# A long convolution with routed experts on one core: fewer half transforms beside the first sort, the rest among the tile tables, rows ahead of the 48-point inputs

## The chip, the core and the metric

The kernel runs on one core of a Trainium2 chip. TensorE (PE), VectorE (DVE), ScalarE (ACT) and GpSimd (POOL) compute, each with an instruction queue of its own; SyncE (SP) issues most of the transfers, GpSimd issues those whose rows are given by a list of indices. The metric is the device time of one execution in microseconds; the lower the better.

## The reference

The input `x` has 8 batches of 5696 positions with 128 channels. Each is convolved with one long filter `h`, and every resulting row goes to the one of 8 experts that its gate prefers:

```python
Yf = np.fft.rfft(x, n=2 * S, axis=1) * np.fft.rfft(h, n=2 * S, axis=0)[None]
y = np.fft.irfft(Yf, n=2 * S, axis=1)[:, :S, :]
...
expert_idx = np.argmax(logits, axis=1)
for e in range(E):
    xe = x[expert_idx == e]
    out[expert_idx == e] = gate_w[expert_idx == e, None] * (np.maximum(xe @ w1[e], 0.0) @ w2[e])
```

Here the rows of `y` are the `x` of the second part, `logits = x @ w_gate`, and an expert has 1024 hidden channels.

## The kernel before

The convolution is a transform in two steps. The first ("half transforms", `phase_a`, tiles `pa`) mixes 120 blocks of a batch by a cosine and a sine matrix and leaves its result in a DRAM tensor `U`; an item is four of 48 columns of one batch, it is split into two float32r parts by ScalarE and VectorE (`xc`), has two halves (cosine, sine) of three matmuls each, and each half is copied out of PSUM to `ut` (one by ScalarE, one by VectorE). Three batches complete one pair of `U` stores. The second step (`phase_b`, 48-point, tiles `xp`, `vp`) takes 120 bins one by one: inputs `uq` from `U`, a matmul forward (`xp`), the product with the filter on VectorE (`zt`, `xs`), a sum (`combine`), and a matmul back (`vp`). `phase_c`, called the sort here, finishes the inverse transform (`lb` in the first group, `yp`), turns the rows (`tp`), scores them (`gb`), ranks them within their expert (`lmax` to `pi`, all on VectorE) and scatters them with GpSimd (`SR<-rt,pi`, line 686) into `SR`, the rows sorted by expert. After each scatter GpSimd clears a scratch tile (`spent`, line 919) in all steps but the last `QUICK`; nothing reads what the clearing writes leave there. `tables` computes, in small VectorE instructions on one partition, which 256 rows of `SR` make up each expert tile (`tab`).

The batches form three groups of 2, 3 and 3. `experts` goes through the tiles of 256 rows: SP reads a tile's place from `tab` and loads its rows (`xr`, line 1126) and, where the expert changes, weights (`wb`, line 1154); TensorE turns the rows (`mx`), multiplies them in four steps by the first weights (`mh`) and the second (`ma`), and GpSimd scatters the result to `out`. The first group's rows make up tiles 0 to 36; tile 37 is the first that needs rows of the second group. Rows are loaded up to three tiles ahead, and only when all scatters of their group are done.

The order of the instructions is planned in the program: `run` advances several generators in step, each with the cost that it yields, divided by its share in `SHARES`. Two stages matter here. In the first, the sort of group 0 (`gather`) runs beside `phase_a` of group 1 (`SHARES[1]`) and the preparation of weights. In the second, `experts` runs beside `rest()` (share 0.75), which goes on with `phase_b`, sort and so on of groups 1 and 2. A generator that yields `None` waits until another has moved on. In `rest()` the pieces of the first table stand two by two behind each bin of `phase_b`, and `begin`, which marks the group's rows as ready, comes when the bins have cost `HEAD[1]`. `LULL` holds the experts for a moment at their start. `ALONE` says for how many bins VectorE, not GpSimd, does the sum.

Of the kernel before, what the change touches and what calls it, by code (L numbers as in the profile page):

```python
# [44 lines left out]
F3 = (False, False, True, False)  # L45
MIX = 2
LD = 4
SHARES = (0.42, 0.195, 0, 0.75, 0.998, 0.42)
GAP = 5000
ALONE = (0, 14, 10)  # L50
HEAD = (0, 5500, 9000)
A3 = (True, True, True, True)
ALO = ('gpsimd', 'vector', 'vector', 'vector')
AT = 650
WARM = 4
TURN = (1, 1, 1, 1)
LULL = 2800
RARE = 3
STEP = 1065
XR = 19  # L60
PACE = (1800, 2200)
ROOM = 28
REST = (224, 288, 288)
QUICK = (1, 1, 24)
TABLED = 4
RATE = (0.372, 0.55, 0.28, 0.8, 1.05, 0.6)

# [2 lines left out]
def conv_moe(ctx: ExitStack, tc: tile.TileContext, I, out, B, S, D, E, F, split):  # L70
# [39 lines left out]
    class Part:  # L110
        def __init__(self, gr, s, b0, nb, c0, tiles):
            self.gr, self.g, self.s, self.b0, self.nb, self.c0 = gr, gr.g, s, b0, nb, c0
            self.cols = nb * D
            self.ni = SLOTS[gr.g] // nb
            while NB % self.ni:
                self.ni -= 1
            self.ns = self.ni * nb
            self.cb = 3 if self.ns % 3 == 0 else 2
            self.cw = self.cb * D
            self.nt = tiles  # L120
            self.ready = False
            self.ends = []
            self.sets = 2 if b0 + nb == B else 1

# [13 lines left out]
    groups, parts = [], []  # L138
# [314 lines left out]
    def phase_b(gr):  # L453
        g, cb, cw, nch, QB, PK = gr.g, gr.cb, gr.cw, gr.nch, gr.qb, gr.pk
# [187 lines left out]
            filt(1, k)  # L642
        for n in range(CUT):
            cut(n)
        for n in range(N + lags[3] + 2):
            qb, at = divmod(n, per)
            for k0 in range(at * PK, (at + 1) * PK):
# [88 lines left out]
    def phase_c(pt, guest=None):  # L736
# [6 lines left out]
        nu = NB // NI  # L743
# [196 lines left out]
        for n in range(n_end + 1):  # L940
            for k in range(nsub):
# [14 lines left out]
                lift(at + 2)  # L956
                if guest:
                    guest.begin(1 if k == nsub - 1 and n >= 1 else 2)
                yield cost if n < nu or pt is parts[-1] else cost / 2
                if guest:  # L960
                    guest.end()
                if n < nu:
# [118 lines left out]
    def begin(pt):  # L1081
        for _ in pt.pieces:
            pass
        pt.ends = lanes[-PIPE_LANES:] + pt.ends
        pt.ready = True

# [22 lines left out]
    def experts():  # L1109
# [118 lines left out]
        def tiles(lo, hi):  # L1228
# [2 lines left out]
            hss, wants, due = {}, [], [lo]  # L1231

            def pump():
                while wants and seq[wants[0][0]][0].ready:
                    load_w(*wants.pop(0))

            def want(i, n):
# [9 lines left out]
                    load(due[0])  # L1247
                    due[0] += 1

            while not seq[lo][0].ready:  # L1250
                yield None
            for n in range(4):
                want(lo, n)
            ahead(lo + 2)
            if lo == 0:
                yield LULL
            M = len(steps)
            for n in range(M + LAG + 1):
                j, k = steps[n] if n < M else (None, None)
# [44 lines left out]
    def gather(pt, guest=None):  # L1304
# [15 lines left out]
        state["space"] = False  # L1320
        yield 0

    def chain(*gens):
        for x in gens:
            yield from x

    def rest():
        wait = [groups[0].parts[-1]]
        for gr in groups[1:]:
            spent = 0  # L1330
            guest = Guest(groups[gr.g + 1]) if gr.g + 1 < len(groups) else None
            bins = phase_b(gr)
            for n, cost in enumerate(bins):
                if guest and n == QN * gr.nch - 12:
                    guest.start()
                spent += cost
                yield cost
                if wait:
                    for _ in range(2):
                        next(wait[0].pieces, None)  # L1340
                    if spent > HEAD[gr.g]:
                        begin(wait.pop())
            for pt in gr.parts:
                yield from gather(pt, guest)
            if guest:
                yield from guest.rest()
                wait.append(gr.parts[-1])
# [26 lines left out]
    with tc.manual_schedule():  # L1374
# [7 lines left out]
        sb.close()  # L1382
        sb.open("c")
        state["rests"] = False
        run((chain(*[gather(pt) for pt in g0.parts]), 1.0), (phase_a(groups[1]), SHARES[1]), (prep, SHARES[5]))
        sb.close()
        sb.close()
        sb.open("sb")
        run((experts(), 1.0), (back, SHARES[3]))
        sb.close()  # L1390


# [76 lines left out]
```

## Time and profile before

| | us |
|---|---|
| device time, median of 3 runs | 2142.5 (2141.74 to 2143.13) |
| the profiled execution | 2141.9, with a span of 2140.1 |
| TensorE busy | 2061.8 (96%) |
| VectorE busy | 1563.6 (73%) |
| GpSimd busy | 1293.2 (60%) |
| ScalarE busy | 1121.1 (52%) |

The span is the time from the first to the last instruction on the core; the device time has a little more around it. TensorE's busy time counts a slow matmul with its full length, so time at the lower clock looks busy.

### The profile page before, as it was taken

To read this page: it belongs to the slowest core of one execution; us is meant where nothing else is said; L and a number is where in the kernel's file an instruction comes from. 1 tells how busy PE (TensorE), PEld (TensorE's weight loads), DVE (VectorE), ACT (ScalarE), POOL (GpSimd) and SP (SyncE) were. 2 spreads that over 40 slices of the span, in tenths; PEclk is the share of its full clock that TensorE was granted. 3 is DMA by queue.
4 is the path that set the end of the run, shared out by engine and by line. 5 is a ranking of instruction groups with operands and counts; after the bars stand their busy time and mean duration, and the time that the engine had idled before them with its cause. 6 is when DMAs were issued, how large, how long until landed. Compare 5 with 4: busy or idle time off the path is not lost.

```text
span 2140.1 us, 47237 instructions
## 1 busy us (share of the span) xinstructions
PE 2061.8 (96%) x14548; PEld 1786.5 (83%) x14548; DVE 1563.6 (73%) x3523; ACT 1121.1 (52%) x2333; POOL 1293.2 (60%) x1431
## 2 busy tenths in 40 slices
PE   9999999799999999989999999999989999999998
PEld 6898777467777777768888888888889999999998
DVE  5688677799998687888888887677774555555554
ACT  5677555155555444435666665444444444444444
POOL 6566388645554288888998776166663444444333
PEclk9999999699999999989999999999999999999999
DMA  8999799889996898868778775656533244443331
GB/s 265 265 274 290 224 305 294 248 208 235 245 241 186 224 282 261 265 153 224 186 188 221 192 192 154 168 135 162 142 101 118 69 130 134 133 132 128 123 122 34
DMA packets 213409, 409.33 MB, mean 191 GB/s; under 512 B 31605, under 2 KB 135339, under 8 KB 213156
## 3 DMA queue, kind: packets, MB, share of 16 engines
q1 hardware_dynamic: 184975, 350.70, 58.6%
q0 software_dynamic: 27072, 55.35, 9.0%
q8 instruction: 118, 1.93, 0.4%
q14 instruction: 135, 1.11, 0.2%
q10 hardware_dynamic: 1109, 0.23, 0.1%
HBM read 571.44 MB, written 154.27 MB: 339 GB/s over the span
## 4 chain that ended last, share of the span: by engine, by line
PE 75%; DVE 7%; DMA 6%; POOL 5%; issue 3%; ACT 2%; SPq 1%; POOLq 0%; DVEq 0%; ACTq 0%
PE mh L164 21%; PE ma L164 21%; PE vp L164 8%; PE xp L164 8%; PE yp L164 4%; POOL SR L686 3%; PE pa L164 3%; PE mx L189 3%; DMA SR<-rt,pi 2%; DMA wb<-WD 1%; POOL spent L919 1%; PE lb L189 1%; PE hp L164 1%; DMA mt<-mq 1%; PE tp L189 1%
## 5 line engine op out<-in xcount | busy, mean ns | idle before, releaser
L1193 DVE SCALAR_TENSOR_TENSOR hs<-mh,hs 128x512 fp32r<-128x512 f32 x728 | 500.7, 689 | 363.0 <-ACT hs L1191 356.8
L164 PE MATMUL mh<-xtb,wb 128*128 128x256 f32 x4368 | 702.9, 296 | 21.6 <-DMA wb<-WD 10.3
L1191 ACT ACTIVATE hs<-mh 128x512 fp32r<-128x512 f32 x728 | 435.4, 598 | 465.6 <-PE mh L164 459.7
L164 PEld LDWEIGHTS mh<-xtb,wb 128*128 128x128 f32 x4368 | 587.2, 189 | 92.1 <-issue 39.3
L164 PE MATMUL ma<-hs,wb 128*128 128x256 f32 x4368 | 656.6, 286 | 7.3 <-DMA wb<-WD 7.2
L164 PEld LDWEIGHTS ma<-hs,wb 128*128 128x128 f32 x4368 | 571.9, 190 | 9.4 <-DMA wb<-WD 9.3
L686 POOL DMA_INDIRECT SR<-rt,pi x384 | 399.2, 1040 | 235.1 <-issue 71.4
L704 POOL DMA_INDIRECT out<-xr x308 | 302.5, 982 | 347.4 <-ACT hs L1191 177.2
L583 POOL TENSOR_TENSOR zt<-zt,xs 128x384 f32<-128x384 f32 (+1 forms) x276 | 295.6, 1073 | 154.3 <-DVE xs L573 74.5
L577 DVE TENSOR_TENSOR xs<-xp,hh 64x384 f32<-64x384 f32 (+1 forms) x360 | 214.7, 596 | 7.8
L620 ACT COPY vt<-vp 96x384 f32<-96x384 f32 x240 | 114.1, 475 | 197.2 <-PE vp L164 191.4
L164 PE MATMUL vp<-zt,mi 128*96 128x384 f32 x480 | 200.2, 499 | 2.0 <-PE xp L164 0.9
L568 DVE TENSOR_TENSOR zt<-xp,hh 128x384 f32<-128x384 f32 (+1 forms) x300 | 173.5, 578 | 31.3 <-PE xp L164 23.2
L164 PE MATMUL xp<-uq,mt 96*128 96x384 f32 (+1 forms) x496 | 175.7, 458 | 8.0 <-DMA uq<-U 4.0
L164 PE MATMUL pa<-xc,fcr 120*120 120x512 f32 x576 | 159.2, 411 | 2.0 <-POOL xc L296 1.0
L164 PE MATMUL yp<-vq,gcs 120*120 120x384 f32 x384 | 140.2, 486 | 2.0 <-ACT ut L329 2.0
L573 DVE SCALAR_TENSOR_TENSOR xs<-xp,hh 64x384 f32<-64x384 f32 x240 | 134.2, 559 | 4.2
L164 PEld LDWEIGHTS vp<-zt,mi 128*96 128x96 f32 x480 | 79.2, 166 | 51.0 <-issue 26.0
L164 PEld LDWEIGHTS pa<-xc,fcr 120*120 120x120 f32 x576 | 99.1, 185 | 25.6 <-DVE rk L908 3.3
L164 PEld LDWEIGHTS xp<-uq,mt 96*128 96x128 f32 x496 | 87.6, 200 | 32.1 <-issue 11.1
L329 DVE COPY ut<-pa 120x512 f32<-120x512 f32 x96 | 65.7, 684 | 64.6 <-PE pa L164 54.8
L557 POOL TENSOR_TENSOR us<-uq,us 96x384 fp32r<-96x384 f32 x81 | 83.0, 1025 | 30.6 <-ACT us L555 29.8
(166 smaller groups left out, 2591.5 us busy)
## 6 DMA issues: line engine op xcount, KB each, us to landing
wb<-WD SPq DMA_DIRECT2D x728, 512.0 KB
U<-ut SPq DMA_DIRECT2D x48, 720.0 KB
uq<-U SPq DMA_DIRECT2D x60, 576.0 KB
V<-vt SPq DMA_DIRECT2D x60, 576.0 KB
vq<-V SPq DMA_DIRECT2D x48, 720.0 KB
xt<-x SPq DMA_DIRECT2D x96, 240.0 KB
xr<-SR SPq DMA_DIRECT2D x154, 130.0 KB
WD<-wsp SPq DMA_DIRECT2D x32, 512.0 KB
```

The source lines that it names most:

```text
L164: nc.tensor.matmul(to, lhs, rhs, **kw)
L189: nc.tensor.transpose(dst, src, ident[:n, :n])
L557: eng.tensor_tensor(out=uv[:, 1], in0=src, in1=uv[:, 0].bitcast(F32), op=ALU.subtract)
L568: nc.vector.tensor_tensor(out=zt, in0=x3, in1=hv[:, 0].broadcast_to([P, PK, cb, D]), op=ALU.mult)
L573: nc.vector.scalar_tensor_tensor(out=xs[to, 0], in0=x3[at, 0], scalar=-1.0, in1=him[:, 0], op0=ALU.mult, op1=ALU.mult)
L577: nc.vector.tensor_tensor(out=xs[to], in0=x3[at], in1=him, op=ALU.mult)
L583: eng.tensor_tensor(out=zt, in0=zt, in1=xs, op=ALU.add)
L620: done = nc.scalar.copy(outs_[qb][:, k0 : k0 + PK, c * cw : (c + 1) * cw], banks.pop(n)[:K2, :iw].rearrange("p (q x) -> p q x", q=PK),)
L686: s = nc.gpsimd.indirect_dma_start(out=SR[:, :], out_offset=IndirectOffsetOnAxis(ap=pi[:, b : b + 1], axis=0), in_=rt[:, b, :], in_offset= ...
L704: sc = nc.gpsimd.indirect_dma_start(out=out[:, :], out_offset=IndirectOffsetOnAxis(ap=xr[:, s, D + 1 : D + 2].bitcast(I32), axis=0), in_=x ...
L1191: done = nc.scalar.activation(hs[:, 0], hp, AF.Relu)
L1193: done = nc.vector.scalar_tensor_tensor(out=hs[:, 1], in0=hp, scalar=0.0, in1=hs[:, 0].bitcast(F32), op0=ALU.max, op1=ALU.subtract)
```

## The change

Beside the first sort the half transforms of group 1 get a share of 0.125 instead of 0.195, and more of them stand beside the sort's last steps (`cost * 2` in the first group). The first table's pieces are given out in that stage (`deal`), one each 1100 ns of planned cost, among the transforms that are left. `experts` starts in that stage as well: with the table known (`tabled`) it issues the first weights. In `rest()`, `begin` comes first, so the first rows are issued ahead of the inputs of the 48-point step, and `phase_b` of group 1 then yields `LEAD` before its first bin, so that experts run some steps ahead. `LULL` goes. Clearing writes stand behind the scatters of the first 8 steps of the first sort instead of the first 15, 42 writes fewer. In group 1 the sum of 2 bins instead of 14 is VectorE's.

```diff
--- before.py
+++ after.py
@@ -45,23 +45,24 @@
 F3 = (False, False, True, False)
 MIX = 2
 LD = 4
-SHARES = (0.42, 0.195, 0, 0.75, 0.998, 0.42)
+SHARES = (0.42, 0.125, 0, 0.75, 0.998, 0.42)
 GAP = 5000
-ALONE = (0, 14, 10)
-HEAD = (0, 5500, 9000)
+ALONE = (0, 2, 10)
+HEAD = (0, 0, 9000)
 A3 = (True, True, True, True)
 ALO = ('gpsimd', 'vector', 'vector', 'vector')
 AT = 650
 WARM = 4
 TURN = (1, 1, 1, 1)
-LULL = 2800
+LEAD = 6400
+DEAL = 1100
 RARE = 3
 STEP = 1065
 XR = 19
 PACE = (1800, 2200)
 ROOM = 28
 REST = (224, 288, 288)
-QUICK = (1, 1, 24)
+QUICK = (8, 1, 24)
 TABLED = 4
 RATE = (0.372, 0.55, 0.28, 0.8, 1.05, 0.6)
 
@@ -118,7 +119,7 @@
             self.cb = 3 if self.ns % 3 == 0 else 2
             self.cw = self.cb * D
             self.nt = tiles
-            self.ready = False
+            self.ready = self.tabled = False
             self.ends = []
             self.sets = 2 if b0 + nb == B else 1
 
@@ -642,6 +643,8 @@
             filt(1, k)
         for n in range(CUT):
             cut(n)
+        if g == 1:
+            yield LEAD
         for n in range(N + lags[3] + 2):
             qb, at = divmod(n, per)
             for k0 in range(at * PK, (at + 1) * PK):
@@ -956,7 +959,7 @@
                 lift(at + 2)
                 if guest:
                     guest.begin(1 if k == nsub - 1 and n >= 1 else 2)
-                yield cost if n < nu or pt is parts[-1] else cost / 2
+                yield cost if n < nu or pt is parts[-1] else cost * (0.5 if g else 2)
                 if guest:
                     guest.end()
                 if n < nu:
@@ -1081,6 +1084,7 @@
     def begin(pt):
         for _ in pt.pieces:
             pass
+        pt.tabled = True
         pt.ends = lanes[-PIPE_LANES:] + pt.ends
         pt.ready = True
 
@@ -1231,7 +1235,7 @@
             hss, wants, due = {}, [], [lo]
 
             def pump():
-                while wants and seq[wants[0][0]][0].ready:
+                while wants and seq[wants[0][0]][0].tabled:
                     load_w(*wants.pop(0))
 
             def want(i, n):
@@ -1247,13 +1251,13 @@
                     load(due[0])
                     due[0] += 1
 
-            while not seq[lo][0].ready:
+            while not seq[lo][0].tabled:
                 yield None
             for n in range(4):
                 want(lo, n)
+            while not seq[lo][0].ready:
+                yield None
             ahead(lo + 2)
-            if lo == 0:
-                yield LULL
             M = len(steps)
             for n in range(M + LAG + 1):
                 j, k = steps[n] if n < M else (None, None)
@@ -1320,12 +1324,19 @@
         state["space"] = False
         yield 0
 
+    def deal(pt):
+        for _ in pt.pieces:
+            yield DEAL
+        pt.tabled = True
+
     def chain(*gens):
         for x in gens:
             yield from x
 
     def rest():
-        wait = [groups[0].parts[-1]]
+        wait = []
+        begin(groups[0].parts[-1])
+        yield 0
         for gr in groups[1:]:
             spent = 0
             guest = Guest(groups[gr.g + 1]) if gr.g + 1 < len(groups) else None
@@ -1382,11 +1393,18 @@
         sb.close()
         sb.open("c")
         state["rests"] = False
-        run((chain(*[gather(pt) for pt in g0.parts]), 1.0), (phase_a(groups[1]), SHARES[1]), (prep, SHARES[5]))
+        work = experts()
+        run(
+            (chain(*[gather(pt) for pt in g0.parts], deal(g0.parts[-1])), 1.0),
+            (phase_a(groups[1]), SHARES[1]),
+            (prep, SHARES[5]),
+            (work, 1.0),
+            stop=(work,),
+        )
         sb.close()
         sb.close()
         sb.open("sb")
-        run((experts(), 1.0), (back, SHARES[3]))
+        run((work, 1.0), (back, SHARES[3]))
         sb.close()
```

Line numbers in the new kernel are up to 18 higher. The following rows are instructions in the order of the program: line, operation, output and inputs, shape, count.

TensorE, behind the last scores of the first sort (`gb_15`) and its last count (`gb_None` with `oh_15`), before:

```order
L164 MATMUL gb_15_None<-c_moe_w_gate,y_110 120x8 x6
L164 LDWEIGHTS ones
L164 MATMUL gb_None_4668<-oh_15_4662,ones 128x54
L164 LDWEIGHTS lt
L164 MATMUL gb_None_4668<-oh_15_4662,lt 120x54
L164 MATMUL xp_0_0_4719<-uq_0_4705,mt_0_4703 128x384
L164 MATMUL xp_1_0_4732<-uq_0_4705,mt_0_4703 128x384
L164 MATMUL xp_2_0_4747<-uq_0_4705,mt_0_4703 128x384
L164 MATMUL xp_3_0_4767<-uq_0_4705,mt_0_4703 128x384
L164 MATMUL xp_4_0_4778<-uq_4_4713,mt_4_4711 128x384
L164 MATMUL vp_0_0_4780<-zt_0_0_4735,mi_118 96x384
```

and now (`pa` are half transforms, `mxNone` turns the first rows, `mh` is the first expert layer):

```order
L165 MATMUL gb_15_None<-c_moe_w_gate,y_110 120x8 x6
L165 MATMUL pa_27_0_4477<-xc_27_4424,fcr 120x512 x3
L165 MATMUL pa_27_1_4483<-xc_27_4424,fcr 120x512 x3
...
L165 MATMUL gb_None_4514<-oh_15_4508,ones 128x54
...
L165 MATMUL gb_None_4514<-oh_15_4508,lt 120x54
L165 MATMUL pa_28_1_4519<-xc_28_4474,fcr 120x512 x3
L165 MATMUL pa_29_0_4529<-xc_29_4492,fcr 120x512 x3
...
L165 MATMUL pa_35_0_4705<-xc_35_4691,fcr 120x512 x3
L165 MATMUL pa_35_1_4710<-xc_35_4691,fcr 120x512 x3
L190 MATMUL mxNone_4767<-ident,xr_4732 128x128 x2
L165 MATMUL mh_0_4773<-xtb_4770,wb_0_0_4661 128x256 x6
```

Before, the 48-point step follows the last count at once; now three more half transforms stand ahead of it and fifteen behind it, then come the experts' first steps, and the first `xp` comes only after 5 of these.

SP, from the last stores of the half transforms (`U`) on, before (`uq`, `mi`, `hh`, `mt` are the inputs of the 48-point step):

```order
L310 DMA U_72<-ut_11_0_4376 120x1536
L310 DMA U_72<-ut_11_1_4422 120x1536
...
L471 DMA mt_0_4703<-mq 96x512
L485 DMA uq_0_4705<-U_72 96x4x384
L488 DMA mi_118<-miq 48x384 x2
L492 DMA hh_115<-HS 48x1024 x2
...
L1140 TENSOR_LOAD tab_4792
...
L1154 DMA wb_0_0_4869<-WD 128x1024
...
L1126 DMA xr_4886<-SR 128x260
```

and now:

```order
L305 DMA xt_35_4608<-x 120x512
L1144 TENSOR_LOAD tab_4630
...
L1158 DMA wb_0_0_4661<-WD 128x1024
...
L1158 DMA wb_0_3_4667<-WD 128x1024
L311 DMA U_72<-ut_10_0_4606 120x1536
L311 DMA U_72<-ut_10_1_4620 120x1536
L311 DMA U_72<-ut_11_0_4689 120x1536
L311 DMA U_72<-ut_11_1_4698 120x1536
...
L1130 DMA xr_4732<-SR 128x260
...
L472 DMA mt_0_4780<-mq 96x512
L486 DMA uq_0_4782<-U_72 96x4x384
```

The table is read ahead of the last four stores, the weights are issued there, and the rows stand between these stores and the inputs of the 48-point step, not behind five sets of inputs.

TensorE at the end of the second sort (last count: `gb_None` with `oh_23`), before:

```order
L164 LDWEIGHTS ones
L164 MATMUL gb_None_12774<-oh_23_12724,ones 128x54
L164 LDWEIGHTS lt
L164 MATMUL gb_None_12774<-oh_23_12724,lt 120x54
L164 MATMUL mh_3_12784<-xtb_12428,wb_0_1_4871 128x256 x6
L164 MATMUL ma_12767<-hs_1_12730,wb_0_2_4873 128x256 x6
L164 MATMUL xp_0_0_12840<-uq_0_12826,mt_0_12824 128x384
L164 MATMUL mh_0_12861<-xtb_12780,wb_0_0_4869 128x256 x6
L164 MATMUL ma_12767<-hs_2_12777,wb_0_3_4875 128x256 x6
L164 MATMUL xp_1_0_12886<-uq_0_12826,mt_0_12824 128x384
...
L189 MATMUL mx_32_12960<-ident,ot_12951 128x128 x2
L189 MATMUL mx_32_12960<-ident,xr_12113 128x128 x2
```

and now:

```order
L165 LDWEIGHTS ones
L165 MATMUL gb_None_13115<-oh_23_13091,ones 128x54
L165 LDWEIGHTS lt
L165 MATMUL gb_None_13115<-oh_23_13091,lt 120x54
L165 MATMUL xp_0_0_13161<-uq_0_13147,mt_0_13145 128x384
L165 MATMUL mh_1_13169<-xtb_13030,wb_0_0_4661 128x256 x6
L165 MATMUL ma_12936<-hs_3_13097,wb_0_3_4667 128x256 x6
L165 MATMUL xp_1_0_13194<-uq_0_13147,mt_0_13145 128x384
L165 MATMUL mh_2_13229<-xtb_13030,wb_0_1_4663 128x256 x6
L190 MATMUL mx_35_13236<-ident,ot_13227 128x128 x2
L190 MATMUL mx_35_13236<-ident,xr_12375 128x128 x2
```

Before, the turn behind the last count takes in tile 32; now it takes in tile 35, so three tiles fewer lie between the second sort and tile 37.

## Rows read from the trace of the kernel before

**Rows 1.** Stretches (us): busy time of each engine, granted PE clock, DMA share, GB/s.

```profile
240.00:380.00 140.00, 138.17 (x771) 107.53 (x770) 101.88 (x299) 83.17 (x183) 98.77 (x145) 1.00 0.92 284
380.00:396.00 16.00, 9.37 (x57) 7.29 (x56) 10.17 (x47) 3.59 (x10) 13.97 (x23) 0.82 0.93 255
396.00:428.00 32.00, 25.24 (x38) 9.85 (x38) 27.08 (x67) 4.19 (x9) 14.74 (x20) 0.55 0.92 261
428.00:460.00 32.00, 30.30 (x155) 21.05 (x156) 30.67 (x57) 17.44 (x35) 9.93 (x10) 1.00 0.84 198
460.00:660.00 200.00, 200.00 (x1092) 148.63 (x1091) 188.66 (x348) 105.66 (x216) 116.29 (x117) 1.00 0.92 238
```

**Rows 2.** PE by time (start, us, instruction, [idle before, releaser]): first handover.

```profile
234.91 2.40 PE L164 MATMUL yp<-hh,gcs 120*120 120x384 f32 x4
...
393.44 0.23 PE L164 MATMUL gb_None<-oh,ones 120*128 120x54 bf16 x1 [1.41 <-DVE sm L890]
...
396.66 4.79 PE L164 MATMUL xp<-uq,mt 96*128 96x384 f32 x8 [2.89 <-DMA uq<-U]
...
427.23 0.63 PE L189 MATMUL mxNone<-ident,xr 128*128 128x128 f32 x2
...
428.32 1.31 PE L164 MATMUL mh<-xtb,wb 128*128 128x256 f32 x6 [0.46 <-ACT xtb L1175]
...
430.77 0.81 PE L164 MATMUL xp<-uq,mt 96*128 96x384 f32 x2
431.41 0.81 PE L164 MATMUL vp<-zt,mi 128*96 128x384 f32 x2
```

**Rows 3.** POOL by time, same columns: first scatter, spacing, last scatter.

```profile
261.46 1.14 POOL L686 DMA_INDIRECT SR<-rt,pi  x1 [27.60 <-DVE wsp L267]
...
393.84 0.99 POOL L686 DMA_INDIRECT SR<-rt,pi  x1 [0.18 <-issue]
394.84 0.29 POOL L919 MEMSET spent<- 120x224 f32 x1
395.32 1.00 POOL L686 DMA_INDIRECT SR<-rt,pi  x1 [0.18 <-DVE cnt L983]
...
411.26 1.00 POOL L686 DMA_INDIRECT SR<-rt,pi  x1 [0.30 <-issue]
412.56 1.00 POOL L686 DMA_INDIRECT SR<-rt,pi  x1 [0.30 <-issue]
```

**Rows 4.** DVE by time, same columns: one subtraction and copy; table's first and last.

```profile
367.39 0.69 DVE L296 TENSOR_TENSOR xc<-xt,xc 120x512 fp32r<-120x512 f32 x1
367.99 0.69 DVE L329 COPY ut<-pa 120x512 f32<-120x512 f32 x1
...
395.02 0.14 DVE L983 TENSOR_TENSOR cnt<-base,c_base 1x8 f32<-1x8 f32 x1
...
415.53 0.15 DVE L1076 TENSOR_TENSOR did<-did,nt 1x8 f32<-1x8 f32 x1
```

**Rows 5.** SP's DMA issues in order of time: start, us, line, transfer, count.

```profile
415.88 2.01 SPq L1154 DMA_DIRECT2D wb<-WD  x4
419.31 2.62 SPq L1126 DMA_DIRECT2D xr<-SR  x3
```

**Rows 6.** The chain that ended last: start, us, what.

```profile
360.73 2.07 PE pa L164 x9
...
391.13 7.46 DMA hh<-HS
```

**Rows 7.** PE at the second handover: last count, first turn with new rows.

```profile
927.92 0.27 PE L164 MATMUL gb_None<-oh,ones 120*128 120x54 bf16 x1
...
1001.64 0.38 PE L189 MATMUL mx<-ident,xr 128*128 128x128 f32 x2
```

**Rows 8.** POOL there: the last scatter of the second sort.

```profile
957.44 1.00 POOL L686 DMA_INDIRECT SR<-rt,pi  x1 [0.30 <-DMA SR<-rt,pi]
```

**Rows 9.** SP there: the first load of the newly sorted rows.

```profile
961.13 0.36 SPq L1126 DMA_DIRECT2D xr<-SR  x1
```

## Prediction

> **What bounds the kernel now.** I read the stretches first [rows 1]. While the first two batches are sorted (240 to 380 us) TensorE is busy 138.17 of 140 us at full clock, and from 460 us, where experts and the next transforms share it, 200.00 of 200. Between lies a hole: 9.37 us busy of 16, then 25.24 of 32 at a granted clock of 0.55, the lower level (1.2 GHz) for nearly all of that time. So TensorE bounds the program, and what is lost in the hole is lost at the end, unless a later hole absorbs it.
>
> TensorE's own timeline says what the hole is made of [rows 2]. Without transforms the last steps of the sort wait for VectorE (the count of 393.44 us for 1.41 us; before 396 us TensorE idles 6.63 us in all, of which about 2.5 are the next wait). Then it waits 2.89 us for the first 48-point input. Until 427 us it does only 48-point work, 18 operations (11 `xp`, 7 `vp`) between waits, and the first expert matmul comes at 428.32 us. The experts were late for three reasons in a row: the tile table ended at 415.7 us on VectorE, because products stood between its pieces [rows 4]; weights went out at 415.88 us and rows at 419.31 us [rows 5]; the last scatter left GpSimd at 413.6 us, 18 us after the last count [rows 3].
>
> **The change, term by term.**
>
> *Sort with fewer transforms.* All 72 half transforms stood ahead of the last count; now 57 do. One costs 0.70 us (9 matmuls, three halves, in 2.07 to 2.1 us on the chain [rows 6]), so 15 of them take 10.5 us out of the sort. The later ones fill the 4.1 us (6.63 less 2.5) that the last steps waited; I take 3.5 back. The last count moves from 393.4 to 379.4 us.
>
> *Tail.* VectorE then has a last rank (five instructions, 1.25 us by the same timeline), the table, five subtractions and seven copies. The table's 33 instructions lie within 20.7 us [rows 4], of which five products, four sums and one wait take 13.7; the table itself is 7.0 us. Copies and subtractions follow each other at 0.60 us [rows 4], so 12 take 7.3. Sum 15.6 us, plus 0.5 for the last transform: the last copy is done at 395.5 us. TensorE has only 10.5 us of work in that time, so VectorE sets the tail. The table ends ahead of the last five of these pieces and a few more, at 390.1 us, against 415.7.
>
> *Clearing writes.* With a write the scatters are 1.48 us apart, without 1.30 [rows 3]. 42 writes go, so 42 x 0.18 = 7.6 us. The 96 scatters cost 48 x 1.48 + 48 x 1.30 = 133.4 us: from 261.5 us to 395 us if nothing holds them, and 406 if the 11 us of stalls in today's 152 us stay. Transforms no longer stretch the sort, so fewer of its ranks come late; I take 398 us, and 400 landed.
>
> *Rows and weights.* SP now sends four weight loads (128 x 1024 floats each) at 391 us, then the last four U stores (120 x 1536 floats each), then rows. That is 5.05 MB ahead of the first rows, with the last scatters 5.5 MB. The small `hh` load, issued at 391.13 us behind U stores and inputs, landed after 7.46 us [rows 6], so loads on this queue do wait for what went ahead. The best rate of [rows 1], 284 GB/s at a share of 0.92, is 309 at a full share: 17.8 us, rows at 408.8 us. The bounds are 255 GB/s, as between 380 and 396 us (21.6 us, 412.6), and no queueing at all (issued at 398.5 us, landed some 2.5 us later, 401). I take the value between them that is nearer the slow end, as the `hh` load is. From the turn to the first expert matmul go 1.1 us (427.23 to 428.32 [rows 2]): 409.9 us. SP waits for the table at that place, with the four U stores behind it and nothing else; the first of them is ready at 391 us too, so the wait costs them little. The first 48-point inputs now go out behind the rows: two of them with their matrices are about 2 MB, 6.5 us at the same rate, landed by 416 us. The first `xp` stands behind five and a half expert steps, some 421 us, so these hide the load; uncovered it would cost those 6.5 us.
>
> The Trainium skill ("DMA: Bandwidth & Descriptors", Queues, rings and completion order) says that each DMA engine takes descriptors of one ring in order, while a copy may run on fewer than 16 rings; it speaks against rows that are issued behind 5 MB. The `hh` load agrees with it. By the rule the experts start at 409.9 us as taken, without it at 402.1.
>
> *What the first handover is worth.* The kernel before had 18 operations done by 428.3 us. At full clock one takes 0.645 us (430.77 to 431.41 [rows 2]), so they are worth 11.6 us: had it started experts at 416.7 us with none of them done, it would stand as well. The new kernel starts at 409.9: 6.8 us gained. It restarts at the lower clock after some 13 us of idling. After a short idle, two `yp` operations of the same width (four matmuls) took 2.40 us at 234.91 [rows 2] instead of 1.29, and the transposes ahead of them lost as much; I charge 2.5 us, and 1 us because `mh_2` waits for a PSUM bank while no other work is at hand. The kernel before lost 1.7 us between 428 and 460 us [rows 1], which experts with 48-point inputs long landed don't. First handover: 6.8 - 3.5 + 1.7 = **5.0 us**.
>
> *Twelve sums move from VectorE to GpSimd.* Nothing: GpSimd has little to do there (9.93 of 32 us [rows 1]), and TensorE bounds what follows. If VectorE were the bound, it would save 12 x 0.57 = 6.8 us.
>
> *Second handover.* Experts now run six steps ahead of the 48-point transforms, so the second sort ends with tile 34 at work instead of 31, and tile 37 is the first that needs new rows. Today 73.7 us pass from the last count to the turn that takes those rows [rows 7], for 55.8 us of TensorE work at full clock (24 expert steps, their turns, 48-point work, counted in the order and priced by full-clock spacing): 17.9 us are lost. In the new order only 22.4 us of work lie between. The rows can't come before the scatters are done, whose last starts 29.5 us after the count [rows 8], with the first load 33.2 us after it [rows 9]; landed and turned, 36. So TensorE waits 13.6 us in one piece and restarts cold for 2.5: 16.1 lost, against 17.9. That is 1.8 us better; scatters may start 2 us earlier against the count, or the restart be worse, so I count **+1.5**, with ends -6 and +4.
>
> *Thinner sort.* Fewer transforms cover fewer waits; 0.5% of 140 us, **-0.7**.
>
> **Sum.** 5.0 + 1.5 - 0.7 = 5.8 us. The profiled execution took 2141.9 us with a span of 2140.1 and stands 0.6 below the median of 2142.5: 2136.1 profiled, **2136.7** as a median.
>
> **Rivals.**
> - *Rows are not held by the queue.* Experts start at 402.1 us, another 7.8 us sooner: 2128.9. For it: rows are small, and a share of the rings may be free. Against: the `hh` load, and scatters may last beyond 402 us. Chance 0.15.
> - *The tail gives it back.* The queue moves 255 GB/s as between 380 and 396 us (3.8 us later), or the second handover costs 4 instead of giving 1.5: a gain of 0 to 2, so 2141. For it: DMA share is 0.92 or more wherever much moves [rows 1]. Chance 0.24.
> - *The sort loses its cover (slower).* TensorE idled 4.1 of about 13.4 us where the sort ran with no transforms. If a sort with a quarter of its transforms moved away loses a tenth of 140 us in the same waits on VectorE, that is 14 us: 2150.7 with the terms above. It ends slower once more than 7% is lost (5.8 + 4.3 us). For it: each rank is a chain of some nine VectorE instructions. Against: the 1.3% that is lost today, and one or two transforms still stand in every step. Chance 0.18.
> - *Nothing happens* is ruled out by the order: rows are issued ahead of the 48-point inputs, and tables stand ahead of products.
>
> **Chances.** Forecast 0.42, rivals as above and 0.01 for anything else. About 0.2%, 4.3 us, is what a measurement of this kernel can tell from no change. The forecast's own range is 2132 to 2140, so some three quarters of it count as faster: with the first rival and a fifth of the second 0.52. Same is the rest of both, 0.29, and slower 0.19. The range for eight in ten reaches to the first rival and most of the way to the last: 2127 to 2149.
>
> **What would show it.** Right: the last count near 380 us; transforms on TensorE until about 395 us; the table's last row near 390 us; rows issued near 398 us; first `mh` at 406 to 413 us with no `xp` ahead of it; full clock some 5 us later; then one idle piece of 10 to 16 us before tile 37's rows are turned. Wrong: a last count later than 385 us (thin sort), a last scatter after 405 us, or a first `mh` after 415 us. I would be most wrong if the second handover idles over 25 us, or if VectorE and not TensorE holds the mixed stretch behind the first.

## The result

| | us |
|---|---|
| predicted | 2136.7 (2127 to 2149) |
| the changed kernel, median of 4 runs | 2163.2 (2162.21 to 2169.87) |
| the kernel before beside it, median of 4 runs | 2142.8 (2141.74 to 2143.43) |
| ratio | 1.0083, 95% interval 1.0060 to 1.0107 |
| the profiled execution | 2163.5, with a span of 2161.7 |

The change makes the kernel 20 us slower. The same stretches as in [rows 1], of the changed kernel (busy time of PE, PEld, DVE, ACT and POOL, granted clock, DMA share, GB/s):

```profile
240.00:380.00 140.00, 136.02 (x776) 106.95 (x775) 102.78 (x341) 80.44 (x178) 106.83 (x139) 0.99 0.89 269
380.00:396.00 16.00, 9.51 (x23) 6.34 (x23) 8.21 (x24) 3.38 (x6) 6.35 (x6) 0.63 0.82 242
396.00:428.00 32.00, 17.62 (x101) 15.65 (x101) 9.75 (x18) 6.05 (x12) 0.00 (x0) 0.70 0.80 215
428.00:460.00 32.00, 29.75 (x162) 21.37 (x162) 31.01 (x58) 14.68 (x31) 17.65 (x18) 1.00 0.78 189
460.00:660.00 200.00, 200.00 (x1095) 148.70 (x1093) 188.52 (x347) 105.91 (x217) 116.09 (x116) 1.00 0.88 234
```

The hole between 380 and 428 us is still there, at a granted clock of 0.63 and 0.70 in the mean, so a good part of it at the lower of the two levels (1.2 GHz). TensorE by time, from the first `yp` of the sort on (answers to [rows 2]):

```profile
230.44 1.52 PE L165 MATMUL yp<-hh,gcs 120*120 120x384 f32 x4
...
371.75 0.20 PE L165 MATMUL gb_None<-oh,ones 120*128 120x54 bf16 x1 [1.25 <-DVE sm L893]
406.42 0.69 PE L190 MATMUL mxNone<-ident,xr 128*128 128x128 f32 x2 [14.07 <-DMA xr<-SR]
417.85 1.23 PE L165 MATMUL mh<-xtb,wb 128*128 128x256 f32 x6 [3.37 <-DMA wb<-WD]
433.44 0.95 PE L165 MATMUL mh<-xtb,wb 128*128 128x256 f32 x6 [2.23 <-DVE hs L1197]
```

The last count comes at 371.8 us and the first expert matmul at 407.6, both earlier than predicted. Part of that isn't the change's work: up to the first `yp` TensorE and SP have the same instructions in the same order in both kernels, and yet it came at 230.44 us here and at 234.91 before [rows 2], 4.5 us apart. In the other runs of the changed kernel and its variants it came between 226.8 and 239.1 us, so this is the spread of single executions. SP's issues (answers to [rows 5]), and VectorE's end of the table and last copies:

```profile
387.02 2.00 SPq L1158 DMA_DIRECT2D wb<-WD  x4
389.12 12.48 SPq L311 DMA_DIRECT2D U<-ut  x4
403.70 4.45 SPq L1130 DMA_DIRECT2D xr<-SR  x4
417.62 0.99 SPq L1158 DMA_DIRECT2D wb<-WD  x3
```

```profile
386.07 0.18 DVE L1065 TENSOR_TENSOR tab<-ej 1x36 int32<-1x36 f32 x1
399.37 1.89 DVE L330 COPY ut<-pa 120x512 f32<-120x512 f32 x3 [10.04 <-DMA U<-ut]
```

At 417.85 us TensorE goes on 0.23 us after SP comes to tile 1's weight loads. These are skipped where the expert stays the same, and 512 KB would take 1.8 us at the best rate of [rows 1], 284 GB/s: TensorE had waited for SP to come past the twelve loads of 48-point inputs and matrices that stand ahead on SP's queue.

The second handover (answers to [rows 7, 9]), the start of the third sort and the third handover, PE by time, with SP's first load of newly sorted rows:

```profile
947.63 0.20 PE L165 MATMUL gb_None<-oh,ones 120*128 120x54 bf16 x1
953.79 1.62 PE L165 MATMUL xp<-uq,mt 96*128 96x384 f32 x2 [5.90 <-DMA uq<-U]
991.08 0.44 PE L190 MATMUL mx<-ident,xr 128*128 128x128 f32 x2 [2.52 <-DMA xr<-SR]
...
1376.65 1.02 PE L165 MATMUL ma<-hs,wb 128*128 128x256 f32 x6 [2.29 <-DMA wb<-WD]
...
1622.05 0.22 PE L165 MATMUL gb_None<-oh,lt 120*120 120x54 bf16 x1
1640.13 1.48 PE L165 MATMUL mh<-xtb,wb 128*128 128x256 f32 x6 [4.76 <-DMA wb<-WD]
1654.71 1.65 PE L165 MATMUL ma<-hs,wb 128*128 128x256 f32 x6 [3.31 <-DMA wb<-WD]
1672.93 0.38 PE L190 MATMUL mx<-ident,xr 128*128 128x128 f32 x2
```

```profile
987.53 2.69 SPq L1130 DMA_DIRECT2D xr<-SR  x3
```

To add such waits up across stages I took, at points of the program, the time plus the TensorE work that is left. Work left is all operations that stand behind that point in the program's order, at their full-clock spacing (0.72 us for six expert matmuls, 0.65 for a 48-point operation or half a `yp`, 0.24 for a `pa` matmul). A stage that wastes nothing leaves the sum as it is; rounded prices give a stage an offset, the same in every kernel, so only differences along a row count. "Second handover" is the 110 us behind the second sort's last count, "start of the third sort" the 65 us around its first `yp`. The columns add up to the spans within 0.5 us. E13 is the changed kernel again, E14 and E15 are experiments below.

| change of the sum, us | before | changed | E13 | E14 | E15 |
|---|---|---|---|---|---|
| the sum at 480 us | 2099.1 | 2097.8 | 2098.0 | 2091.9 | 2097.6 |
| mixed stretch | -0.8 | -0.2 | -0.1 | +2.6 | +2.2 |
| second sort | +23.8 | +22.7 | +23.8 | +16.2 | +18.6 |
| second handover | +17.2 | +24.3 | +24.1 | +19.3 | +20.8 |
| second mixed stretch | -0.2 | +1.4 | +0.8 | +0.8 | -0.8 |
| start of the third sort | +0.1 | +6.4 | +5.7 | +0.2 | +0.3 |
| rest of the third sort | +9.0 | +10.6 | +9.4 | +12.6 | +12.5 |
| third handover and end | -8.0 | -0.8 | -3.0 | -9.3 | -9.5 |

Behind the first handover the changed kernel is 1.3 us ahead; without the 4.5 us by which its first `yp` came earlier it is 3.2 us behind (E13, by the same reckoning, 0.2 behind). It loses 7.1 us in the second handover, 6.3 at the start of the third sort and 7.2 in the third handover against before, 20.6 of the 22 us by which the profiled executions differ. One execution tells a stage only to a few us: E13 and E14, with the same program up to the sixth expert step, have their first expert matmul at 408.7 and 403.3 us.

### The profile page after: what moved, and what is told of

Read it like the earlier page. It is cut to its first block, busy times and chain, and to the rows that moved or that the text cites. A ratio compares the mean times of both kernels' runs of the same rounds, so it can differ in the third digit from the quotient of the medians.

```text
span 2161.7 us, 47176 instructions
## 1 busy us (share of the span) xinstructions
PE 2059.5 (95%) x14548; PEld 1791.8 (83%) x14548; DVE 1558.1 (72%) x3511; ACT 1120.4 (52%) x2333; POOL 1291.6 (60%) x1401
## 5 line engine op out<-in xcount | busy, mean ns | idle before, releaser
L165 PE MATMUL mh<-xtb,wb 128*128 128x256 f32 x4368 | 714.1, 299 | 25.8 <-DMA wb<-WD 12.8
L165 PEld LDWEIGHTS ma<-hs,wb 128*128 128x128 f32 x4368 | 574.6, 191 | 14.1 <-DMA wb<-WD 13.9
L584 POOL TENSOR_TENSOR zt<-zt,xs 128x384 f32<-128x384 f32 (+1 forms) x288 | 306.6, 1066 | 138.7 <-DVE xs L574 88.2
L165 PE MATMUL vp<-zt,mi 128*96 128x384 f32 x480 | 195.5, 488 | 0.7 <-DVE xs L574 0.7
L165 PE MATMUL xp<-uq,mt 96*128 96x384 f32 (+1 forms) x496 | 169.1, 443 | 5.9 <-DMA uq<-U 5.9
L165 PE MATMUL pa<-xc,fcr 120*120 120x512 f32 x576 | 165.8, 421 | 6.7 <-DVE xc L297 3.4
```

Source lines behind the costliest of these rows:

```text
L165: nc.tensor.matmul(to, lhs, rhs, **kw)
L584: eng.tensor_tensor(out=zt, in0=zt, in1=xs, op=ALU.add)
```

## The experiments

Theory A: the lead costs it. The experts stand 3 tiles (12 steps) further ahead of the other work, so that fewer tiles are left to cover each later handover. Theory B: the other edits cost it (fewer transforms beside the sort, fewer clearing writes, sums on GpSimd). Theories C and D are on SP's order in the first handover.

The kernel before took 2142 and 2144 us beside E5 to E8 and E13 to E16 (one chip), but 2217 to 2239 beside the rest, on two other chips; comparisons are therefore only made within a group that ran together.

**The pause in one piece, and LEAD itself (E1 to E8).** The pause is this edit of `experts`, at tile 6, at tile 40 in E2 and E7, and with 27000 in E8:

```diff
-                yield 1420
+                yield 1420 + (17000 if (j, k) == (6, 0) else 0)
```

> The changed kernel, with one addition: at the seventh tile, in the middle of the mixed stretch in which TensorE has no gaps, the experts pause for 17000 ns of planned cost (12 steps). Everything up to some 480 us stays as it is; from then on experts and 48-point work stand to each other as in the kernel before (tile 31 instead of 34 at the second sort's last count, 95 instead of 98 at the third's). By time plus work left, the changed kernel is 1.5 us ahead of the kernel before behind the first handover, and loses about 7 us in the second handover, 5 to 7 at the start and in the course of the third sort, and 6 to 7 in the third handover. Theory A (the lead of the experts costs it: fewer tiles are left to cover each handover): nearly all of that comes back, 2141 us (2138 to 2145). Theory B (the other edits cost it: thinner sort, scatters without clearing writes, 12 sums moved to GpSimd): nothing comes back, 2163 us (2160 to 2166).

> The same pause of 17000 ns, at tile 40, so behind the second handover: that one stays as in the changed kernel, the third sort and third handover see the relation of the kernel before. Theory A: the 12 to 14 us lost behind 1340 us come back and the 7 us of the second handover do not, about 2150 us (2147 to 2154). Theory B: 2163 us.

E3 and E4 set `LEAD = 0` and `LEAD = 12800`.

> The changed kernel with LEAD 0: the experts are ahead by 6 of the 12 to 14 steps less (tile 33 at the second sort's last count, 96 at the third's). Theory A with a loss that grows evenly with the lead: half of it comes back, about 2153 us (2148 to 2158). Theory B: 2163 us, or worse, since 48-point inputs are then needed at once behind the first rows.

> The changed kernel with LEAD 12800: the experts are ahead by 6 steps more at the second sort's last count (tile 36, and tile 37 is the first that needs new rows), by 3 at the start of the third sort and 2 at its end. Theory A: the second handover costs some 6 us more and the later ones 1 or 2, about 2170 us (2166 to 2176). Theory B: 2163 us.

Measured beside the kernel before at 2217.2 us: E1 2251.1 (ratio 1.0144, 1.0116 to 1.0172), E2 2249.5 (1.0135, 1.0114 to 1.0156), E3 2244.2 (1.0108, 1.0086 to 1.0130), E4 2253.6 (1.0150, 1.0126 to 1.0175). The order by lead, E3 under E4, is A's, and by the same sums E4 loses 10 us more than E3 in the second handover. The rest is open without the changed kernel on that chip, so the pauses ran again with it:

> The changed kernel as it is, beside the next three on one chip. The first four runs stood on a chip on which the kernel before itself took 2217 us, so the changed kernel's time there isn't known, and nothing can be subtracted. Both theories: 0.8% above the kernel before, as measured at first, if this chip is like the first one; on a chip like that of the first four runs the kernels there stood 1.1 to 1.5% above.

> The pause of 17000 ns at the seventh tile again (the lead is given back behind the first handover). Theory A (the lead costs the time): some 20 us under the changed kernel and level with the kernel before, ratio 0.998 to 1.002. Theory B (other edits cost it): as the changed kernel.

> The pause at tile 40, behind the second handover. Theory A: 12 to 14 us under the changed kernel, 7 us above the previous one. Theory B: as the changed kernel.

> The pause at the seventh tile with 27000 ns instead of 17000: experts stand 7 steps further back than in the kernel before (tile 29 instead of 31 at the second sort's last count, 93 instead of 95 at the third's), so that two more tiles cover each handover. Theory A, with losses that go on shrinking: some 3 to 8 us under the kernel with 17000. Theory A with a floor (what is left to lose are stalls that cover doesn't help): level with it. Theory B: as the changed kernel.

Beside the kernel before at 2141.7: E5 2163.1 (1.0112, 1.0087 to 1.0138), E6 2165.1 (1.0115, 1.0093 to 1.0137), E7 2156.3 (1.0073, 1.0048 to 1.0098), E8 2158.4 (1.0075, 1.0051 to 1.0100). E6 missed A's number by 23 us; by its time alone it is where B had it. E7 came 6.8 us under E5, where A said 12 to 14, and E8 6.8 under E6, within A's 3 to 8. The pause itself shows a reason, in the stretches in which it stands (E6, then E8):

```profile
480.00:520.00 40.00, 33.85 (x115) 17.75 (x114) 38.34 (x70) 18.70 (x37) 23.75 (x24) 1.00 0.98 239
```

```profile
480.00:540.00 60.00, 50.21 (x173) 26.55 (x172) 57.65 (x105) 27.33 (x55) 34.89 (x35) 1.00 0.99 246
```

With 48-point work alone (from 485 to 516 us in E6) VectorE is busy 38.3 of 40 us, the DMA engines have a share of 0.98, and TensorE idles 6.2, in E8 9.8 of 60. Which of the two holds it there is not shown; a share of the waits ends with a 48-point input. By the sum of time and work left E6's mixed stretch costs 7.4 us, and its second sort 8 more than E5's, while the second handover (+19.4), the start of the third sort (+0.3) and the third handover (-8.3) come out near the kernel before. (E6's profiled execution lay 9 us under its median.) So the lead had to be given back without a gap.

**The lead given back bit by bit (E9, E14), and SP's order (E10, E11).**

```diff
-                yield 1420
+                yield 1420 + (190 if 6 <= n < 96 and lo == 0 else 0)
```

> The changed kernel with 190 ns more of planned cost on each of 90 expert steps of the first mixed stretch: the lead is given back bit by bit (tile 31 at the second sort's last count, 95 at the third's, as before), where the pause in one piece left 48-point work alone for 16 us and cost 8 to 12 us by itself. By time plus work left, the pauses had brought back 4 us in the second handover, 5 at the start of the third sort and 8 in the third handover. Theory A (lead): with no gap in the mixed stretch the whole of it is seen, 2144 us on a chip where the kernel before takes 2142 (2141 to 2150). Rival (VectorE, 94% busy in that stretch, turns into the bound when more 48-point work stands in it): 2150 to 2156 with idle TensorE between 440 and 700 us. Theory B (other edits cost the time): 2162 us.

E10 splits `LEAD` in `phase_b` of group 1, E11 has both edits:

```diff
+        if g == 1:
+            yield LEAD / 2
         for qb in range(3 if g == 0 else 2):
             load_m(qb)
...
         if g == 1:
-            yield LEAD
+            yield LEAD / 2
```

> The changed kernel with half of LEAD ahead of the first 48-point loads instead of behind them: on SP's queue the first of tile 1's conditional weight loads then stands ahead of these inputs. In the changed kernel TensorE waits 3.37 us at tile 1 for it, and goes on 0.23 us after SP has reached it. Theory C (that wait, and the second cold restart behind it, come from SP's order): the wait shrinks to under 1 us and the start gains 2 to 5 us, 2158 to 2161 us. Rival (the inputs, issued later, are then late by as much): no change, 2163 us, with a wait for a 48-point input at 424 us.

> Both edits of the two runs above together. Theories A and C: their gains add up, 2139 to 2145 us, about level with the kernel before. If only A holds, as with the first edit alone.

E12 puts two constants back, `QUICK = (1, 1, 24)` and `ALONE = (0, 14, 10)`:

> The changed kernel with QUICK 1 and ALONE 14 as before: 42 clearing writes and 12 VectorE sums are back. Theory A (lead alone): no change, 2160 to 2166 us, since SP issues the rows only at 403.7 us, behind the last U stores, 17 us after the last scatter has started; 7.6 us more of writes fit in there. Theory B (these edits cost the time): 2142 to 2155 us.

Beside the kernel before at 2223.5: E9 2234.5 (1.0052, 1.0023 to 1.0080), E10 2253.1 (1.0141, 1.0082 to 1.0201), E11 2233.8 (1.0041, 1.0018 to 1.0064), E12 2252.3 (1.0107, 1.0047 to 1.0168). The two with the lead given back stand 18 to 19 us under the two with it, as A says, and their traces say it in A's three places: E10 and E12 lose 4.4 to 7.9 us more than E9 and E11 in the second handover, 6.7 to 7.4 at the start of the third sort and 4.9 to 5.9 in the third handover. But E9 and E11 stay 10 to 11 us over the kernel before, above A's ranges, so on this chip the lead isn't all; the first sort is the other part, see E17. The rival with VectorE is out: E9's first mixed stretch loses 2.8 us, E10's 1.5 and E12's 2.8. The clearing writes and sums of E12 change nothing in the time that its interval, some 27 us wide, would show. In E10 the wait for weights at the first step of tile 1 is gone (E9 and E12 have 3.2 and 2.7 us there), but it comes back at that tile's third step, again behind 48-point inputs on SP's queue, which reaches those weights at 440.87 us:

```profile
441.09 0.95 PE L165 MATMUL mh<-xtb,wb 128*128 128x256 f32 x6 [2.22 <-DMA wb<-WD]
```

So SP's order was the cause of the wait, as C says, but the edit moved it and left 2.2 us of it, where C had under 1, and no time is gained. The first of the edits again, with its control:

> The changed kernel as it is, the control of the next three: 0.8 to 1.1% above the kernel before.

> The lead given back bit by bit (190 ns on each of 90 expert steps). Theory A: 16 to 19 us under the changed kernel on the same chip (4 to 6 in the second handover, 4 to 5 at the start of the third sort, 7 to 8 in the third handover). Theory B: level with it.

E15 loads the first weights behind the last `U` stores:

```diff
     def deal(pt):
         for _ in pt.pieces:
             yield DEAL
-        pt.tabled = True
```

> As the run before, but the first weights are loaded when the rows are, behind the last four U stores on SP's queue (the table no longer releases them); TensorE's order is the same. Theory D (SP's wait for the table holds the U stores, these hold VectorE's last copies 10 us, and rows are issued behind both): the transforms' last stores go out some 5 us earlier, rows are issued near 396 us, not 404, and the first expert matmul starts 2 to 4 us earlier; 2 to 4 us under the run before. Rival (5 MB of weights and stores must move ahead of the first rows in any order): first expert matmul and time unchanged, or 1 to 3 us later, since the weights are now last.

E16 has all three edits.

> As the run before, with half of LEAD ahead of the first 48-point loads, so that tile 1's first weight check stands ahead of them on SP's queue. Theory C: another 2 to 4 us, which with D would bring it level with the kernel before or under it (2137 to 2142 on the first chip). Rival: no difference, since the inputs are then later.

Beside the kernel before at 2144.0: E13 2160.8 (1.0087, 1.0061 to 1.0112), E14 2146.2 (1.0009, 0.9991 to 1.0027), E15 2139.3 (0.9978, 0.9960 to 0.9996), E16 2141.0 (0.9997, 0.9980 to 1.0014). Giving the lead back returns 14.7 us of the 16.8, a little under A's 16 to 19, and the table above shows it in A's three places: 4.8, 5.5 and 6.3 us of E14 against E13. E14's profiled execution lay 10 us under its median, so these sizes are rough. At the start of the third sort and in the third handover E15 and E16 agree with it; in the second handover they bring back 3.3 and 1.2 us only. The third handover, the worst 20 us of E13 and then of E14:

```profile
1640.00:1660.00 20.00, 14.90 (x103) 14.29 (x103) 8.99 (x22) 6.03 (x12) 0.12 (x1) 0.87 0.31 102
```

```profile
1600.00:1620.00 20.00, 16.62 (x126) 16.27 (x125) 10.36 (x25) 7.76 (x16) 2.14 (x3) 0.91 0.20 58
```

E13's hole is deeper, and the 20 us ahead of it are hardly better (15.45 us busy); beside E14's stand 19.99 and 18.71. Theory D fell. In E15 SP sends the weights behind the stores:

```profile
386.57 9.58 SPq L311 DMA_DIRECT2D U<-ut  x4
398.41 3.04 SPq L1158 DMA_DIRECT2D wb<-WD  x4
402.59 3.77 SPq L1130 DMA_DIRECT2D xr<-SR  x4
```

The rows are issued at 402.6 us, not 396, and turned at 409.7. From the end of the last transform to the first expert matmul pass 15.7 us in E15, 15.0 in E14, 14.1 in E13: the rival, 5 MB in any order, holds. E15's gain in time over E14, 6.9 us between the medians, is at the edge of the intervals and not explained by D. E16, with C's edit as well, is not under E15: C's 2 to 4 us did not come.

**The lead alone, in the kernel before (E17).** The edit of E9 with the other sign (1230 for 1420 on 90 steps), in the kernel before:

> The kernel before with one edit: 90 expert steps of the first mixed stretch cost 1230 instead of 1420 ns in the plan, so that the experts gain 12 steps on the 48-point work, bit by bit (tile 34 instead of 31 at the second sort's last count, 98 instead of 95 at the third's: the lead of the changed kernel). First handover, sort, clearing writes and sums are those of before. Theory A (the lead alone costs it): 15 to 19 us over the kernel before (ratio 1.007 to 1.009), lost in the second handover, at the start of the third sort and in the third handover. Theory B (it takes the other edits as well): level with the kernel before, 0.998 to 1.002.

Beside the kernel before at 2238.7: 2251.7, ratio 1.0076 (1.0047 to 1.0106): the ratio is A's, the 13.0 us between the medians are a little under its 15 to 19. So the lead costs time without any of the other edits. And E15 again in that group:

> The run with the lead given back and the first weights behind the last stores again: ratio 0.9978 (0.9960 to 0.9996) the first time. If that was more than chance, 0.996 to 0.9996 again; if it was chance, about 1.001, as without the edit to the weights.

2251.9, ratio 1.0062 (1.0041 to 1.0084): the 0.2% did not come again on another chip. No version here beats the kernel before on every chip.

E17 has the first stage of the kernel before with the lead, E18 that of the changed kernel without it, on one chip and within 0.3 us of each other. Their traces set the two apart. At the start of the third sort and in the third handover E17 loses 6.7 and 5.9 us more, as A says; in the second handover it loses no more. At 480 us, however, E18 is 15 us behind. There the first sort is the cause: between its first and last count TensorE idles 18.1 us in E18 and 9.6 in E17, and 14.6 to 17.5 in E1 to E4 and E9 to E11. On the chip of E5 to E8 and E13 to E16 it idles 1.7 to 3.6 there, and 6.2 in the trace of the kernel before. E12, the one variant with the old number of clearing writes, idles 6.8 on the slower chip. So on the two slower chips theory B holds in part, beside A: by the sums the first sort loses 8 to 14 us more there than in E17. That the missing clearing writes are the reason is likely, but rests on E12 and E17 alone and wasn't tested by itself.

## Why the prediction was wrong, step by step

- **Sort with fewer transforms, tail, thinner sort.** Right in direction, a little too small in size: the last count came at 371.8 us (379.4 predicted), the table was complete at 386.9 (390.1), the last half transform ended at 392.3 (close to 395). From the first `yp` to the last count passed 141.3 us against 158.5 before, 17.2 less where 14.0 were taken; the other 4.5 us are the earlier start. TensorE idled 4.0 us of the 140 up to 380 us (1.8 before [rows 1]), not 14: the slower rival as I drew it is not what happened in this run. On the two slower chips it did, with the 14.6 to 18.1 us above.
- **Clearing writes, rows and weights.** The last scatter started at 386.9 us, where I took its end for 398, and that bought nothing: SP issued the rows at 403.7. I had said that SP's wait for the table costs the stores behind it little. In fact the stores held `ut`, VectorE's last copies waited 10.0 us for it, and the rows stood behind all of it. The total, 5 MB ahead of the rows, still gave a time near the forecast (turned at 406.4, first expert matmul at 407.6 against 409.9; counted from the first `yp` 2.1 us later than forecast). The rule of the Trainium skill ("DMA: Bandwidth & Descriptors", Queues, rings and completion order), that each engine takes a ring's descriptors in order, agrees with two rows: rows behind stores whose issue had taken 12.5 us were turned 2.7 us after their issue, rows right behind 2 MB of weights (E15) 7.1 us after it.
- **What the first handover is worth: 5.0 us.** This step failed. The head start looks larger than worked out (9.1 us by time plus work left at the first expert matmul, 6.8 taken), but 4.5 of it were there before the change could act; 4.6 are left (6.7 in E13). And the restart cost 10.1 us, not 3.5: the lower clock, 3.37 us for SP at tile 1's weight check, 2.23 us for VectorE's `hs`. The kernel before lost 2.3 us there, of which I had counted 1.7. So 4.6 - 10.1 + 2.3 = -3.2 us, not +5.0; the 1.3 us by which the profiled execution is ahead are luck of its start.
- **Twelve sums.** Taken as nothing; E12's interval is too wide to test it.
- **Second handover: +1.5, with ends -6 and +4.** This step failed, beyond its lower end: -7.1. I had TensorE wait 13.6 us in one piece for the rows and lose 2.5 to a cold restart, 16.1 in all against 17.9 before. From the last count to the turn that takes tile 37's rows pass 43.4 us, not 36. TensorE idles 14.8 of them, near what I took, but in seven pieces: the longest is 5.9 us for a 48-point input, and only the last, 2.5 us, is for the rows. What I mis-sized is the clock. The rest of the time above the 22.6 us of work, 6.1 us, goes into matmuls at the lower level (granted clock 0.84 in the mean), and behind the turn 1.6 us of idling and 2.1 of slow matmuls follow: 8.2 us in place of 2.5, and 24.7 lost in all. The kernel before loses 17.9 there, 10.6 of it idle, and nothing behind the turn. The rows were late as well: the last scatter started 29.3 us after the count, as predicted (29.5), but they were issued 39.9 us after it and not 33.2. The tile table was complete only 34.3 us after the count (27.5 before), and the load stands behind the weight checks of tile 36 on SP's queue, which SP passes only as TensorE finishes its steps (last row below). So tiles that run ahead don't get their rows early; they wait in line with their own steps.
- **What the sum left out: the third sort and the third handover.** I counted the lead's price in one place only. A lead of 3 tiles stays to the end of the third sort. At its start 6.3 us are lost, with TensorE waiting for weights among experts (3.6 us in all; the row at 1376.65 us is the longest wait). And between the third sort's last count and tile 104, the first with rows of the last part, only 6 tiles are left instead of 9: 45 groups of six expert matmuls and their turns, some 35 us of work, within 50.9 us, against 71 groups, some 55 us, within 64.1 before. So 16 us are lost there, 9 before. The two places make 13.5 us of the 20, and neither the sum nor a rival had them.

From the last count to the turn with new rows, second handover before and now, then third handover before and now (columns as in [rows 1]):

```profile
927.92:1001.64 73.72, 63.11 (x379) 52.92 (x379) 63.62 (x140) 31.29 (x64) 59.13 (x71) 0.92 0.75 196
947.63:991.08 43.45, 28.63 (x152) 22.43 (x151) 34.90 (x89) 11.97 (x24) 36.42 (x48) 0.84 0.76 196
1587.34:1651.46 64.12, 57.55 (x464) 56.21 (x463) 38.45 (x91) 26.40 (x53) 26.94 (x28) 0.97 0.32 98
1622.05:1672.93 50.88, 40.46 (x297) 39.41 (x296) 28.11 (x73) 16.95 (x35) 17.08 (x17) 0.90 0.36 103
```

The third handover before, PE by time, and SP's longest wait between 976 and 990 us of the changed kernel (us in total, times, longest; it ended at 985.6 us):

```profile
1587.34 0.21 PE L164 MATMUL gb_None<-oh,lt 120*120 120x54 bf16 x1
1651.46 0.38 PE L189 MATMUL mx<-ident,xr 128*128 128x128 f32 x2
```

```profile
SPq L1158 <- PE mh L165: 3.5, 1, 3.5
```

What stays open: how much of the second handover the lead itself costs (E15, E16 and E17 show less than E14 does); why the start of the second sort, too, came out 7.6 us better in E14 than in E13, and the wait for `uq` (5.9 us behind the last count), which E14 has as well (5.7) and the kernel before has not.

## What to carry to other kernels

A stage that starts earlier keeps its lead: before counting the head start as a gain, go to every later place where that stage waits for another, and count how much work is left as cover there. A conditional load that is skipped still stands in the issuing queue, and whoever waits for it waits for all that is queued ahead of it. To take a lead back, spread it: in one piece it leaves TensorE alone with work whose other engines or transfers were only just hidden. And before reading a gain off two traces, compare them at the last point up to which the programs are the same.

## What the runs showed of the hardware

The same kernel took 2142 to 2144 us on one chip and 2217 to 2239 on two others, where the two ends of that range come from one chip at two times. Most of it is lost in the third sort: of the 97 us between the traces of E13 and E12 (which differ in two constants as well) the rest of the third sort, by time plus work left, holds 60. Both between 1440 and 1680 us:

```profile
1440.00:1680.00 240.00, 226.29 (x1892) 200.60 (x1891) 165.86 (x541) 101.87 (x236) 140.53 (x135) 0.99 0.52 135
```

```profile
1440.00:1680.00 240.00, 203.37 (x1555) 167.51 (x1554) 134.55 (x464) 80.67 (x196) 122.19 (x118) 0.93 0.45 114
```

In E12 ScalarE alone waits 30.3 us there for something that the profile puts outside the core's own engines and queues (`remote`); E13 has no such wait. Such waits stand in all ten traces from the two slower chips and in none of the other ten. In the first sort, from 300 to 400 us, VectorE's copies to `hh` wait so for 8.5 to 18.7 us in eight of the ten; the two without are E12 and E17, which have the old number of clearing writes. E12 from 1440 to 1680 us, and E18 from 300 to 400 us (us in total, times, longest):

```profile
ACT hs L1195 <- remote: 30.3, 5, 7.0
```

```profile
DVE hh L785 <- remote: 15.3, 2, 10.0
```

What it is was not settled.
